# Issuing one small ones-matmul in front of a long V product instead of behind it, in a cached attention decode step

## The chip, the cores and the metric

The kernel runs on one core of one Trainium2 chip. The metric is the device time of one execution in microseconds (us). The profile's span of one execution is about 1.8 us shorter than that time. The record marks each run fast or slow by its time and granted clock.

## The reference, cut to what matters

```python
def _A_ref(x, k_cache, v_cache, wq, wo):      # B=2, Sq=1, D=512, 32 heads of Dh=128, Sk=8192, bf16
    q = (x @ wq) as heads
    scores = einsum("bhqd,bhkd->bhqk", q, k_cache) * (Dh ** -0.5)
    p = softmax(scores)
    o = einsum("bhqk,bhkd->bhqd", p, v_cache)
    return o as one row @ wo
h  = x + _A_ref(layernorm(x), ...)
h2 = h + gated_mlp(layernorm(h))              # F=1376
```

There is one query row for each of two batch rows, so every byte of the K and V caches (2 x 134 MB) is read once and used for very little arithmetic.

## The kernel before

The work is a loop over 32 "pairs": a pair is two heads of one batch row, 16 pairs to a row. Each pair has a K tile and a V tile of 4 MB each. All tiles come through one ring of 6 buffers, loaded by one issuing queue (SyncE).

```python
    def scores(n, between=None):               # VectorE, in place in the K tile
        ...
        nc.vector.tensor_tensor(out=kt, in0=kt, in1=qb, op=ALU.mult)
        if between is not None:
            between()
        width = Dh
        while width > 8:                       # four halving additions, then a reduction
            ...
        ... exp on ScalarE into pm[n % 3]; its sums go to zm[:, b, i, :]

    def weighted_v_moving(n):                  # TensorE: 32 matmuls on the V tile
        ...
        for g in range(T2 // TG):
            nc.tensor.matmul(out=o, lhsT=pm[...], rhs=vt[...], ...)
        ... copy by ScalarE, then 4 small matmuls into ob[b][:, i, :]

    def inverse_z(b, s, e):
        zb = ps_s.tile([P, e - s, 2], f32, tag="st", name="zb")
        nc.tensor.matmul(out=zb, lhsT=mean_f, rhs=zm[:, b, s:e, :], start=True, stop=True)
        nc.vector.reciprocal(out=zi[b][:, s:e, :], in_=zb)

    def first_row():                           # normalize batch row 0
        inverse_z(0, 0, NP)
        normalize(0, 0, NP, ob[0])

    load_k(0)
    for n in range(N - 2):                     # N = 32, NP = 16
        load_k(n + 1)
        load_v(n)
        scores(n, between=first_row if n == NP + 2 else None)
        weighted_v_moving(n)
```

The softmax denominators of batch row 0 are summed over partitions by `zb`, a matmul with a matrix of equal constants (the ones-matmul of the title). VectorE uses it in the middle of pair 18, between that pair's multiply and its additions. In TensorE's program order `zb` stands behind the V product of pair 17.

The softmax here doesn't subtract the row's maximum and nothing guards it: scores larger than these inputs give would overflow.

## Time and profile before

| | before |
|---|---|
| time, median | 667.52 us (667.27 to 667.75) |
| VectorE busy | 596.5 us, 90% of the span |
| TensorE busy | 340.3 us, 51% |
| queue of loads, packets' time | 99.1% of 16 engines' span |
| moved | 281.35 MB, mean 423 GB/s |

Two readings compete. These are rows of the page's forty equal slices (about 16.6 us each; a digit is the busy share in tenths) and the head of its chain of waits.

```profile
DVE  1699999999999999999999479999999999999941
...
DMA  9999999999999999999999999999999999999996
...
DVE 71%; DMA 22%; PE 4%; issue 2%; SPq 1%; ACT 0%; DVEq 0%; ACTq 0%
```

VectorE (DVE) has one visible hole, two slices wide, and the chain puts 71% on VectorE. Read alone, this says: VectorE is the limit, so fill the hole. The DMA row says something else: it never falls below 9 until the last slice. The list of VectorE's waits (total us, times, longest us) gives the hole a name:

```profile
DVE kv L173 <- DMA kv<-in_A_k_cache_dram: 17.7, 7, 13.7
DVE zi_224 L225 <- PE zb L224: 13.0, 1, 13.0
```

And this is TensorE's timeline around it (start us, duration us, then the instruction; in brackets the idle time before it and what ended it):

```profile
364.73 1.05 PE L213 MATMUL ob_221<-sel,osb 8*128 8x2 f32 x8 [0.74 <-ACT osb L211]
374.13 9.82 PE L207 MATMUL o<-kv,pm_87 128*8 128x512 bf16 x32 [8.35 <-DMA kv<-in_A_v_cache_dram]
384.69 1.05 PE L213 MATMUL ob_221<-sel,osb 8*128 8x2 f32 x8 [0.74 <-ACT osb L211]
385.67 0.41 PE L224 MATMUL zb<-zm,mean_f 128*128 128x32 f32 x2
```

TensorE idles 8.35 us for V of pair 17, multiplies for 9.82 us, and only then comes to `zb`, 0.41 us of work whose inputs were ready earlier. The Trainium skill, "PSUM — Partial Sum Buffer", section "Engine vs sequencer instructions", says that matmuls start and complete in program order; this trace agrees: `zb` starts at 385.67 us, behind the product. VectorE's multiplies and the reciprocal show the price:

```profile
344.95 8.69 DVE L173 TENSOR_TENSOR kv<-kv,qrep 128x16384 bf16<-128x16384 bf16 x1 [0.66 <-DMA kv<-in_A_k_cache_dram]
364.39 8.69 DVE L173 TENSOR_TENSOR kv<-kv,qrep 128x16384 bf16<-128x16384 bf16 x1 [0.66 <-DMA kv<-in_A_k_cache_dram]
386.11 0.36 DVE L225 RECIPROCAL zi_224<-zb 128x32 f32<-128x32 f32 x1 [13.02 <-PE zb L224]
396.58 8.68 DVE L173 TENSOR_TENSOR kv<-kv,qrep 128x16384 bf16<-128x16384 bf16 x1
415.27 8.68 DVE L173 TENSOR_TENSOR kv<-kv,qrep 128x16384 bf16<-128x16384 bf16 x1
```

In the six pairs up to the stall the starts are 19.44 us apart, with a short wait for K each time (earlier, VectorE catches up with the loads at 18.69 us a pair). After the stall they are 18.69 us apart, without a wait. The first figure is the pace of the loads, the second is VectorE's own. The table by stretches (start:end, length, busy us of PE, PEld, DVE, ACT and POOL with counts, granted clock, DMA share, GB/s) covers the time before, around and after the stall:

```profile
14.00:364.39 350.39, 181.93 (x734) 74.36 (x730) 332.76 (x108) 28.04 (x93) 0.00 (x0) 0.72 1.00 431
364.39:396.58 32.19, 12.25 (x50) 5.54 (x50) 18.92 (x9) 1.68 (x6) 0.00 (x0) 0.63 1.00 431
396.58:602.00 205.42, 111.02 (x440) 44.96 (x440) 202.78 (x67) 15.24 (x55) 0.00 (x0) 0.73 1.00 431
```

In the middle stretch VectorE is busy for 18.92 of 32.19 us, yet the loads run at the same 431 GB/s as everywhere else.

### The profile page before, as it was taken

To read this page: it belongs to the slowest core of one execution; us is meant where nothing else is said; L and a number is where in the kernel's file an instruction comes from. 1 tells how busy PE (TensorE), PEld (TensorE's weight loads), DVE (VectorE), ACT (ScalarE), POOL (GpSimd) and SP (SyncE) were. 2 spreads that over 40 slices of the span, in tenths; PEclk is the share of its full clock that TensorE was granted. 3 is DMA by queue.
4 is the path that set the end of the run, shared out by engine and by line. 5 is a ranking of instruction groups with operands and counts; after the bars stand their busy time and mean duration, and the time that the engine had idled before them with its cause. 6 is when DMAs were issued, how large, how long until landed. Compare 5 with 4: busy or idle time off the path is not lost.

```text
span 665.8 us, 4530 instructions
## 1 busy us (share of the span) xinstructions
PE 340.3 (51%) x1930; PEld 152.9 (23%) x1930; DVE 596.5 (90%) x221; ACT 53.2 (8%) x176; POOL 1.6 (0%) x11
## 2 busy tenths in 40 slices
PE   2344356654445665444656524656554445654284
PEld 1211122211122221112222111222211212212274
DVE  1699999999999999999999479999999999999941
ACT  2200000000000000000000000000000000000010
POOL 0000000000000000000000000000000000000000
PEclk9756787666678866677787568787765788766655
DMA  9999999999999999999999999999999999999996
GB/s 378 439 424 427 441 431 418 441 435 422 433 431 429 432 433 429 429 439 428 425 437 426 428 439 427 428 435 439 416 434 441 419 430 439 423 436 426 380 398 235
DMA packets 15020, 281.35 MB, mean 423 GB/s; under 512 B 1204, under 2 KB 5400, under 8 KB 6040
## 3 DMA queue, kind: packets, MB, share of 16 engines
q1 hardware_dynamic: 14996, 281.06, 99.1%
q8 instruction: 15, 0.25, 0.1%
q14 instruction: 5, 0.04, 0.0%
q10 hardware_dynamic: 4, 0.00, 0.0%
HBM read 281.05 MB, written 0.00 MB: 422 GB/s over the span
## 4 chain that ended last, share of the span: by engine, by line
DVE 71%; DMA 22%; PE 4%; issue 2%; SPq 1%; ACT 0%; DVEq 0%; ACTq 0%
DVE kv L179 34%; DVE kv L173 32%; DMA kv<-in_A_v_cache_dram 18%; DVE sc L187 4%; DMA kv<-in_A_k_cache_dram 3%; PE o L207 3%; SPq L159 1%; PE y_ps L326 0%; PE gate_ps L308 0%; PE up_ps L308 0%; PE o_b L219 0%; PE ob_221 L213 0%; DVE y_row L336 0%; PE ln2mu L99 0%; PE yt_ps L334 0%
## 5 line engine op out<-in xcount | busy, mean ns | idle before, releaser
L173 DVE TENSOR_TENSOR kv<-kv,qrep 128x16384 bf16<-128x16384 bf16 x32 | 277.9, 8684 | 17.7 <-DMA kv<-in_A_k_cache_dram 17.7
L179 DVE TENSOR_TENSOR kv<-kv 128x8192 bf16<-128x8192 bf16 (+3 forms) x128 | 276.2, 2158 | 4.3
L207 PE MATMUL o<-kv,pm_85 128*8 128x512 bf16 x320 | 92.3, 460 | 100.8 <-DMA kv<-in_A_v_cache_dram 60.9
L207 PE MATMUL o<-kv,pm_86 128*8 128x512 bf16 x320 | 92.6, 461 | 83.7 <-DMA kv<-in_A_v_cache_dram 67.6
L207 PE MATMUL o<-kv,pm_87 128*8 128x512 bf16 x320 | 89.3, 449 | 83.9 <-DMA kv<-in_A_v_cache_dram 67.9
L207 PEld LDWEIGHTS <-pm_85 128*8 128x8 bf16 x320 | 31.7, 100 | 157.6 <-issue 68.2
L207 PEld LDWEIGHTS <-pm_86 128*8 128x8 bf16 x320 | 31.9, 100 | 140.2 <-issue 74.9
L207 PEld LDWEIGHTS <-pm_87 128*8 128x8 bf16 x320 | 31.2, 98 | 137.8 <-issue 74.5
L211 ACT ACTIVATE osb<-o 8x512 f32<-8x512 f32 x30 | 17.6, 586 | 409.4 <-PE o L207 409.4
L187 DVE TENSOR_REDUCE sc<-kv 128x128 f32<-128x1024 bf16 x32 | 39.0, 1219 | 3.6 <-DVE kv L179 0.5
L213 PE MATMUL ob_220<-sel,osb 8*128 8x2 f32 x128 | 16.8, 248 | 11.8 <-ACT osb L211 11.8
L213 PEld LDWEIGHTS ob_220<-sel,osb 8*128 8x128 f32 x128 | 15.4, 186 | 19.9 <-ACT osb L211 18.6
L213 PE MATMUL ob_221<-sel,osb 8*128 8x2 f32 x112 | 14.7, 249 | 10.3 <-ACT osb L211 10.3
L213 PEld LDWEIGHTS ob_221<-sel,osb 8*128 8x128 f32 x112 | 13.5, 186 | 17.4 <-ACT osb L211 17.4
L192 ACT ACTIVATE pm_85<-sc 64x128 bf16<-64x128 f32 x22 | 7.6, 344 | 66.7 <-DVE sc L187 66.6
L192 ACT ACTIVATE pm_86<-sc 64x128 bf16<-64x128 f32 x22 | 7.6, 344 | 60.3 <-DVE sc L187 60.2
L139 PE MATMUL qps<-wq_sb,xnb 128*64 128x512 bf16 x64 | 9.4, 464 | 5.1 <-DMA wq_sb<-in_A_wq_dram 5.1
L225 DVE RECIPROCAL zi_224<-zb 128x32 f32<-128x32 f32 x1 | 0.4, 358 | 13.0 <-PE zb L224 13.0
L267 PEld LDWEIGHTS <-wo_sb 128*128 128x128 bf16 x256 | 8.9, 118 | 10.3 <-DMA wo_sb<-in_A_wo_dram 8.7
L192 ACT ACTIVATE pm_87<-sc 64x128 bf16<-64x128 f32 x20 | 6.9, 345 | 37.9 <-DVE sc L187 37.7
L267 PE MATMUL a_ps<-oc_222,wo_sb 128*128 128x1 bf16 x128 | 4.4, 172 | 8.5 <-DMA wo_sb<-in_A_wo_dram 8.5
L219 PEld LDWEIGHTS <-kv 128*128 128x128 bf16 x256 | 7.4, 105 | 4.7 <-issue 2.9
(73 smaller groups left out, 64.6 us busy)
## 6 DMA issues: line engine op xcount, KB each, us to landing
kv<-in_A_k_cache_dram SPq DMA_DIRECT2D x32, 4096.0 KB, 35.2
kv<-in_A_v_cache_dram SPq DMA_DIRECT2D x31, 4096.0 KB, 43.9
wq_sb<-in_A_wq_dram SPq DMA_DIRECT2D x1, 4096.0 KB, 12.5
wo_sb<-in_A_wo_dram SPq DMA_DIRECT2D x1, 4096.0 KB, 46.7
kv<-in_A_v_cache_dram SPq DMA_DIRECT2D x4, 1024.0 KB, 20.2
wgu<-in_B_W_gate_dram SPq DMA_DIRECT2D x1, 1376.0 KB, 27.3
wgu<-in_B_W_up_dram SPq DMA_DIRECT2D x1, 1376.0 KB, 27.2
wd_sb<-in_B_W_down_dram SPq DMA_DIRECT2D x1, 768.0 KB
```

The source lines that it names most:

```text
L139: nc.tensor.matmul(out=qps[half * HALF:(half + 1) * HALF], lhsT=xnb[:, b, c, :], rhs=wq_v[:, c, g * QP:(g + 1) * QP, half, :], start=(c == ...
L159: nc.sync.dma_start(out=t[:, j * step:(j + 1) * step, :], in_=src[:, j * step:(j + 1) * step, :])
L173: nc.vector.tensor_tensor(out=kt, in0=kt, in1=qb, op=ALU.mult)
L179: nc.vector.tensor_tensor(out=_view(kt, 0, [[Dh, T2], [1, half]]), in0=_view(kt, 0, [[Dh, T2], [1, half]]), in1=_view(kt, half, [[Dh, T2], ...
L187: nc.vector.tensor_reduce(out=sc, in_=_view(kt, 0, [[Dh, T2], [1, 8]]), axis=AXIS.X, op=ALU.add)
L192: nc.scalar.activation(out=pm[ps, :, half], in_=sc[ps, :], func=ACT.Exp, accum_out=zm[ps, b, i, half:half + 1], scale=SCALE)
L207: nc.tensor.matmul(out=o, lhsT=pm[:, ts, :].rearrange("p t two -> p (t two)"), rhs=vt[:, ts, :].rearrange("p t d -> p (t d)"), start=(g == ...
L211: nc.scalar.activation(out=osb, in_=o, func=ACT.Copy)
L213: nc.tensor.matmul(out=ob[b][:, i, :], lhsT=osb[:, j, :], rhs=sel[:, j, :], start=(j == 0), stop=(j == TG - 1))
L219: nc.tensor.matmul(out=o, lhsT=vt[:, t, :], rhs=pm[:, t, :], start=(t == 0), stop=(t == T2 - 1))
L225: nc.vector.reciprocal(out=zi[b][:, s:e, :], in_=zb)
L267: nc.tensor.matmul(out=a_ps[:, b, c:c + 1], lhsT=wo_v[:, h, :, c], rhs=oc[b][:, h // 2, h % 2:h % 2 + 1], start=(b == 0 and h == 0 and c = ...
```

## The change

The intent is to let the ones-matmul run in the time in which TensorE waits for V of pair 17 anyway, so that VectorE finds the sum ready in pair 18. Nothing is added or removed.

```diff
-    def inverse_z(b, s, e):
+    def sum_z(b, s, e):
         zb = ps_s.tile([P, e - s, 2], f32, tag="st", name="zb")
         nc.tensor.matmul(out=zb, lhsT=mean_f, rhs=zm[:, b, s:e, :], start=True, stop=True)
-        nc.vector.reciprocal(out=zi[b][:, s:e, :], in_=zb)
+        return zb
+
+    def inverse_z(b, s, e, zb=None):
+        nc.vector.reciprocal(out=zi[b][:, s:e, :], in_=zb or sum_z(b, s, e))
 ...
     def first_row():
-        inverse_z(0, 0, NP)
+        inverse_z(0, 0, NP, zb0)
 ...
         scores(n, between=first_row if n == NP + 2 else None)
+        if n == NP + 1:
+            zb0 = sum_z(0, 0, NP)
         weighted_v_moving(n)
```

## The prediction

> **What bounds the kernel now.** The load queue, over nearly the whole run, although VectorE looks busy (90% in the table of engines). The page's DMA part: 281.35 MB, queue packets filling 99.1% of sixteen engines' time. The table by stretches gives 431 GB/s at a DMA share of 1.00 in all three of: 14 to 364.39 us (before the stall that the change aims at), 364.39 to 396.58 us (around it), 396.58 to 602 us (after it). The stall does not show in the DMA. The Trainium skill, "DMA: Bandwidth & Descriptors", section "Where 436 GB/s comes from", puts the fabric's ceiling at 435.2 GB/s; 431 measured agrees, so there is no reserve.
>
> A pair is 8.39 MB, so 19.45 us at 431 GB/s (estimate). VectorE needs 18.69 us a pair (timeline; starts 396.58, 415.27, 433.95). From 248 to 364 us it starts each multiply after a 0.66 us wait for K, every 19.44 us: the load pace.
>
> **What the change touches.** VectorE has multiplied pair 18 by 373.1 us and then waits 13.0 us (list of waits) for the ones-matmul zb. That stands on TensorE behind pair 17's 32 V matmuls, which start when that V lands at 374.13 and last to 384, then the ScalarE copy (0.59) and 8 small matmuls (1.05); zb itself takes 0.41 us at 385.67. The change adds no instruction, byte or buffer. It puts zb right after the small matmuls that end at 365.8, into TensorE's 8.35 us idle before V of pair 17 lands. The first row's z is long complete. So the wait of 13.0 us goes to about 0; reciprocal (0.36) and normalize (0.19) stay. V products are not delayed.
>
> **How much is critical.** The chain of waits does not run through the stall here, but through two V loads of 48 us and their products. In before, the stall lets loads get ahead: after it VectorE runs 13 pairs at 18.69 without waiting for K. After the change it meets K just in time and waits about 0.7 us a pair, some 9 us over 13 pairs, given back. Its last multiply would start near 364.4 + 13 x 19.44 = 617.1 instead of 620.9 us, 3.8 us earlier. This does not shorten the end: the last V quarter lands at 651.0 us, 11 us after VectorE's last pair (639.6), then comes a fixed tail. Its landing is set by the bytes queued ahead. At 384 to 397 us several 4 MB loads are still queued, so the delayed issues never empty the queue; issuing earlier only makes loads wait longer in it.
>
> **Prediction.** 667.3 us, range 665.0 to 669.0 (before 667.52). Faster by over 2%: 0.03; within 2%: 0.95; slower by over 2%: 0.02.
>
> **What would show it.** Right: the zi wait of 13.0 us disappears; VectorE's wait for K grows from 17.7 us in 7 waits to 25 to 28 in about 20; multiply starts stay 19.4 us apart after pair 18; GB/s stays 431 in each stretch; median K issue-to-landing time grows from 35 towards 45 us; the last V quarter lands at 651 within 1 us. VectorE's last multiply starts 2 to 4 us earlier, without effect.
>
> Wrong: if the DMA rate rises above 431 after 396 us and the last V lands several us earlier, loads had reserve and the stall was critical; up to 13 us could go (654). If zb still waits (a dependence on the newest z accumulate or its PSUM buffer), nothing moves. If the deeper queue disturbs the order at the end (gate, up and down weights behind V), the tail could lengthen by 1 to 2 us.

## The result, and the profile after

The changed kernel takes 667.37 us (median, 667.23 to 667.40), against 667.52 us. The ratio is 0.9997 with a 95% interval of 0.998 to 1.0015. Ratios here are the mean time of one kernel's fast runs over that of the other's of the same rounds, so they are not quite the ratio of the medians.

The local effect is exactly what was intended. On TensorE, `zb` now runs at 364.90 us, and pair 17's product starts when its V lands, as before:

```profile
364.90 0.41 PE L224 MATMUL zb<-zm,mean_f 128*128 128x32 f32 x2
374.27 8.87 PE L207 MATMUL o<-kv,pm_87 128*8 128x512 bf16 x32 [8.96 <-DMA kv<-in_A_v_cache_dram]
```

VectorE's wait for `zb` in row 0 is gone from the list of waits, and the wait for K has grown from 17.7 us in 7 waits to this:

```profile
DVE kv L173 <- DMA kv<-in_A_k_cache_dram: 27.3, 21, 13.6
```

The reader sees the time going back in the starts of the multiplies:

```profile
364.53 8.69 DVE L173 TENSOR_TENSOR kv<-kv,qrep 128x16384 bf16<-128x16384 bf16 x1 [0.66 <-DMA kv<-in_A_k_cache_dram]
373.14 0.35 DVE L228 RECIPROCAL zi_224<-zb 128x32 f32<-128x32 f32 x1
383.98 8.69 DVE L173 TENSOR_TENSOR kv<-kv,qrep 128x16384 bf16<-128x16384 bf16 x1 [0.30 <-DMA kv<-in_A_k_cache_dram]
403.42 8.69 DVE L173 TENSOR_TENSOR kv<-kv,qrep 128x16384 bf16<-128x16384 bf16 x1 [0.66 <-DMA kv<-in_A_k_cache_dram]
422.86 8.69 DVE L173 TENSOR_TENSOR kv<-kv,qrep 128x16384 bf16<-128x16384 bf16 x1 [0.66 <-DMA kv<-in_A_k_cache_dram]
```

There is no hole any more, but the spacing is 19.44 us almost to the end (once it is 20.73). The last multiply starts at 618.79 instead of 620.85 us: of the 13 us only 2.1 arrive there, and they are of no use, because the kernel ends with the last quarter of V, which reaches TensorE at 651.14 us instead of 651.02. The first two lines are from before, the last two from after:

```profile
620.85 8.68 DVE L173 TENSOR_TENSOR kv<-kv,qrep 128x16384 bf16<-128x16384 bf16 x1
651.02 0.35 PE L219 MATMUL o_b<-pm_86,kv 128*128 128x2 bf16 x7 [1.67 <-DMA kv<-in_A_v_cache_dram]
...
618.79 8.69 DVE L173 TENSOR_TENSOR kv<-kv,qrep 128x16384 bf16<-128x16384 bf16 x1 [0.76 <-DMA kv<-in_A_k_cache_dram]
651.14 0.34 PE L219 MATMUL o_b<-pm_86,kv 128*128 128x2 bf16 x7 [1.86 <-DMA kv<-in_A_v_cache_dram]
```

Here is the same table by stretches, and the same rows of the page:

```profile
14.00:364.39 350.39, 179.70 (x738) 73.90 (x735) 332.74 (x108) 28.79 (x96) 0.00 (x0) 0.73 1.00 431
364.39:396.58 32.19, 13.70 (x55) 5.82 (x55) 31.47 (x10) 1.72 (x7) 0.00 (x0) 0.71 1.01 434
396.58:602.00 205.42, 110.88 (x434) 44.88 (x433) 194.17 (x66) 15.24 (x55) 0.00 (x0) 0.71 1.00 431
```

```profile
DVE  1699999999999999999999999999999998999931
...
DMA  9999999999999999999999999999999999999996
...
DMA 48%; DVE 47%; SPq 1%; PE 1%; issue 1%; DVEq 0%; ACT 0%
```

The chain of waits has changed from 71% VectorE and 22% DMA to 47% and 48%, while the time has not moved. Two resources whose paces differ by 4% (19.44 against 18.69 us a pair) each wait for the other somewhere, and following the chain back one step at a time jumps between them on waits of 0.66 us. Its shares are then no measure of what a saving is worth.

Loads are issued earlier and wait longer: the median time from issue to landing grew from 35.2 to 39.5 us for K and from 43.9 to 48.6 us for V.

### The profile page after: what moved, and what is told of

It is laid out like the page before. It is cut to its first block, busy times and chain, and to the rows that moved or that the text cites. A ratio compares the mean times of both kernels' runs of the same rounds, so it can differ in the third digit from the quotient of the medians.

```text
span 665.6 us, 4528 instructions
## 1 busy us (share of the span) xinstructions
PE 340.4 (51%) x1930; PEld 152.9 (23%) x1930; DVE 597.7 (90%) x221; ACT 53.2 (8%) x176; POOL 1.6 (0%) x11
## 2 busy tenths in 40 slices
DMA packets 15020, 281.35 MB, mean 423 GB/s; under 512 B 1204, under 2 KB 5400, under 8 KB 6040
## 4 chain that ended last, share of the span: by engine, by line
DMA 48%; DVE 47%; SPq 1%; PE 1%; issue 1%; DVEq 0%; ACT 0%
DMA kv<-in_A_k_cache_dram 45%; DVE kv L179 22%; DVE kv L173 22%; DMA kv<-in_A_v_cache_dram 4%; DVE sc L187 3%; SPq L159 1%; PE y_ps L331 0%; PE gate_ps L313 0%; PE up_ps L313 0%; PE o_b L219 0%; DVE y_row L341 0%; PE ln2mu L99 0%; PE yt_ps L339 0%; PE ln2var L108 0%; PE a_ps L272 0%
## 5 line engine op out<-in xcount | busy, mean ns | idle before, releaser
L173 DVE TENSOR_TENSOR kv<-kv,qrep 128x16384 bf16<-128x16384 bf16 x32 | 278.0, 8688 | 27.3 <-DMA kv<-in_A_k_cache_dram 27.3
L139 PEld LDWEIGHTS <-xnb 128*64 128x64 bf16 x64 | 5.1, 123 | 8.2 <-issue 5.0
## 6 DMA issues: line engine op xcount, KB each, us to landing
kv<-in_A_k_cache_dram SPq DMA_DIRECT2D x32, 4096.0 KB, 39.5
kv<-in_A_v_cache_dram SPq DMA_DIRECT2D x31, 4096.0 KB, 48.6
wgu<-in_B_W_up_dram SPq DMA_DIRECT2D x1, 1376.0 KB, 27.3
```

Of the source, the lines that this page charges most:

```text
L139: nc.tensor.matmul(out=qps[half * HALF:(half + 1) * HALF], lhsT=xnb[:, b, c, :], rhs=wq_v[:, c, g * QP:(g + 1) * QP, half, :], start=(c == ...
```

## The experiments

Theory A: the load queue works at its full rate all the time and sets the end; a pause of VectorE costs nothing as long as enough loads are queued and VectorE can catch up. Rival B: VectorE's time is critical, and the 13 us were lost elsewhere. Rival C: what limits the loads is not their bandwidth but how soon buffers come free.

### More pause: 21 and 42 extra reductions (e1, e2)

The pause is put back as work with thrown-away results, after the multiply of pair 18. It is longer than the old stall. The diff is cut: `junk` is a scratch tile.

```diff
         if between is not None:
             between()
+            if n == NP + 2:
+                for _ in range(21):        # 42 in e2
+                    nc.vector.tensor_reduce(out=junk, in_=_view(kt, 0, [[Dh, T2], [1, 8]]),
+                                            axis=AXIS.X, op=ALU.add)
```

> The changed kernel with 21 extra reductions of 1.22 us on VectorE (25.6 us, results thrown away) where the old stall was; the outputs stay right. Theory A (the load queue sets the end; a pause of VectorE is absorbed as long as loads are queued): VectorE loses 25.6 us at pair 18 but stops waiting for K for the rest, 8 to 9 us back; its last multiply starts near 633.5, its end (652) just passes the landing of the last V (651), so the time grows by 1 to 6 us, to 668 to 673; GB/s stays 431 until 600 us. Rival B (VectorE's time is critical, and the change's gain was lost elsewhere): 25 us more, near 693.

> The same with 42 extra reductions, 51 us. Theory A: about 30 us of loads lie queued ahead of the next one, so the queue now runs empty for some 15 to 25 us and VectorE ends long after the last V: 690 to 702, that is 23 to 35 us for 51 us of added work, and a visible fall of GB/s near 400 us. Rival B: 51 us more, near 719.

The 21 reductions took 26.3 us, and the kernel took 676.58 us: 9.1 us more than before. The 42 took 52.6 us, and the kernel 703.02 us: 35.5 us more, 1.0 us over the top of what was expected. Neither is what rival B says (the full 26 and 52 us). Between the two, 26.3 us of work cost 26.4 us, so past some knee every microsecond is paid. If a pause below the knee costs nothing, these two points put it at about 26.3 - 9.1 = 17.2 us of pause (an estimate, checked in e8), some 4 us more than the old stall of 13.0 us.

The table by stretches shows that in e1 the loads did not notice (lines of 374 to 414 us):

```profile
374.00:384.00 10.00, 9.75 (x32) 3.19 (x31) 9.73 (x9) 0.00 (x0) 0.00 (x0) 0.72 1.00 429
...
404.00:414.00 10.00, 3.12 (x8) 0.97 (x9) 9.79 (x6) 0.80 (x4) 0.00 (x0) 0.51 1.01 436
```

In e2 the queue did run dry, 40 to 50 us into a pause that began at 373.6 us:

```profile
404.00:414.00 10.00, 0.00 (x0) 0.00 (x0) 9.73 (x9) 0.00 (x0) 0.00 (x0) 0.50 1.00 429
414.00:424.00 10.00, 0.00 (x0) 0.00 (x0) 9.73 (x9) 0.00 (x0) 0.00 (x0) 0.50 0.66 285
424.00:434.00 10.00, 0.00 (x0) 0.00 (x0) 9.86 (x5) 0.00 (x0) 0.00 (x0) 0.50 0.00 0
434.00:444.00 10.00, 6.44 (x22) 2.27 (x23) 9.49 (x4) 0.80 (x4) 0.00 (x0) 0.64 0.68 263
```

So the queue holds out for well over 40 us without VectorE, more than the 30 us expected: TensorE finished pair 17 in the pause and freed one more buffer, and a K load went out at 384.0 us. What sets the knee is therefore not the queue running empty, but VectorE's own way to the end, and the tail on TensorE that follows it (e8, e9): with 26.3 us of pause VectorE never waits for K again and runs at 18.69 us a pair up to 653.3 us, after the last V has landed.

The larger miss is that of e1. There the last multiply starts at 634.16 us as expected (633.5), but 676.58 us is 3.6 us above the top of what was expected. The experiments e9 and e10 below ask why.

### The knee, checked (e8)

The same edit, with 13 reductions.

> 13 extra reductions at pair 18, 1.252 us each as measured in the 21-reduction run, so 16.3 us. From the two delay runs (26.3 us cost 9.1 us, 52.6 us cost 35.5 us, so every us past the knee is paid in full) the knee is at about 17.2 us. Theory A with that knee: 667.2 to 668.0, still free, with the last multiply of VectorE near 624.1. If instead the cost rises smoothly from zero (a share of every stall is paid): about 3 to 5 us, 670 to 672.

Measured: 668.57 us, ratio 1.0017 (1.0004 to 1.0029), for a pause of 16.3 us. The last multiply starts at 624.31 us, as expected. The total is 0.6 us over the top of the expectation and 1.4 us under the bottom of the smooth alternative, so the cost stays small up to the knee. The trace shows where the rest lies. In e8 TensorE no longer waits for the last V; it reaches the last 25 matmuls of the final V product at 651.35 us, and in the kernel before, where it does wait for V, at 651.37 us. So at 16.3 us VectorE's path has just drawn level with the loads. The excess of this trace is a gap that follows, for which the profile shows no releaser (first before, then e8):

```profile
652.67 0.81 PE L219 MATMUL o_b<-pm_86,kv 128*128 128x2 bf16 x25 [1.30 <-issue]
...
653.57 0.80 PE L223 MATMUL o_b<-pm,kv 128*128 128x2 bf16 x25 [2.22 <-issue]
```

The spans differ by 0.9 us (666.7 and 665.8), as the gaps do. e1 fits as well: its last multiply starts 9.85 us later than in e8, its gap is 0.60 us, and its span is 8.2 us longer, which is 9.85 less the 1.62 by which the gap is shorter. Read from the traces, the knee is thus at about 16 us, some 3 us above the old stall. Why the gap varies was not investigated. It stands at a fixed place: in the kernel before, the tail has gaps of 1.28, 1.51 and 1.30 us without a releaser, with 128 matmuls from each to the next. That TensorE waits there for its instructions (the page lists an instruction queue of 15 packets, 0.25 MB) is a guess that no run tested.

### Order on TensorE in the tail (e9, e10)

At the end of the kernel the same kind of ones-matmul stands in front of the V product of pair 30. It needs the last exponentials; the product does not.

```diff
-    inverse_z(L, NP - 1, NP)
     o_a = ps_o.tile([P, 1, 2], f32, tag="o", name="o_a")
     weighted_v_stationary(N - 2, o_a[:, 0, :], 0, T2)
+    inverse_z(L, NP - 1, NP)
     normalize(L, NP - 2, NP - 1, o_a)
```

> The 21-reduction kernel with the last pair's ones-matmul issued behind the V product of pair 30 instead of in front of it. The first 21-reduction run took 676.6 us, 3.6 us over the top of what was expected, because VectorE's end is followed by a serial tail in which that V product (3.41 us, 128 matmuls) waits in TensorE's order behind a ones-matmul that needs the last exponentials. If that explains the miss, 672.8 to 673.8 now. If the rest of the tail absorbs it, 676.6.

> The changed kernel with the same reorder at its end and no extra work. There the last V quarter lands at 651.1 us, after that product is done (644), so under theory A the time stays: 667.2 to 667.6. If the order on TensorE in the tail counts even here, up to 3.4 us faster, 664.

With the pause of e1, the reorder brought 676.58 down to 673.36 us, inside what was expected. TensorE's timeline of e1, and then of e9:

```profile
654.18 0.59 PE L228 MATMUL zb<-zm,mean_f 128*128 128x2 f32 x2 [6.94 <-ACT pm L196]
654.63 3.55 PE L223 MATMUL o_a<-pm,kv 128*128 128x2 bf16 x128
```

```profile
647.01 3.16 PE L223 MATMUL o_a<-pm,kv 128*128 128x2 bf16 x113
...
654.09 0.59 PE L228 MATMUL zb<-zm,mean_f 128*128 128x2 f32 x2 [1.31 <-ACT pm L196]
```

In e1 the product of pair 30 sits behind a wait of 6.94 us; in e9 it runs inside that wait. This accounts for 3.2 of the 3.6 us by which e1 missed. It also moves the knee: with this order the same pause costs 673.36 - 667.41 = 5.95 us instead of 9.1 (667.41 is e10, below). Without the pause (e10) the same reorder gave 667.41 us, ratio 0.9998 (0.9986 to 1.0011): nothing, because the last V quarter lands after that product either way. This is the studied change in small: a reorder on TensorE is worth its time only where the path that it shortens, and not the load queue, ends last.

### Less work for VectorE (e3)

The first of the four halving additions is left out, so VectorE sums half of the products. The arithmetic is wrong; the comparison with the reference passed all the same, so it says nothing about this part.

```diff
-        width = Dh
+        width = Dh // 2
```

> The changed kernel without the first of the four halving additions (4.44 us a pair, 142 us in all; the scores are then of half of the products only, so the output is wrong on purpose). VectorE needs 14.25 us a pair. Theory A: the time stays, 665 to 668, and VectorE's wait for K grows by over 100 us. Rival B: far faster, below 600.

Measured: 667.57 us, ratio 1.0000 (0.9983 to 1.0016). VectorE's busy time fell from 597.7 to 457.1 us, 141 us less, and not one of them reached the total. They went here:

```profile
DVE kv L173 <- DMA kv<-in_A_k_cache_dram: 159.8, 30, 13.4
```

This is the plainest verdict against rival B.

### Fewer bytes, in both orders (e4, e5)

The V loads of pairs 20, 22, 24 and 26 are left out; those products read the spent K tile. The output is wrong, and the comparison passed here too. The edit also holds those K tiles until their products are done, in both kernels alike. e4 has the changed order, e5 the order before.

```diff
+    SKIP = (20, 22, 24, 26)
 ...
-        load_v(n)
+        if n in SKIP:
+            vts[n] = kts[n]
+        else:
+            load_v(n)
```

> The changed kernel with the V loads of pairs 20, 22, 24 and 26 left out (16.8 MB, 38.9 us at 431 GB/s; those products read the spent K tile instead, so the output is wrong on purpose). VectorE's work is unchanged. Theory A: with the queue relieved the end is set by VectorE, running at 18.69 us a pair from about pair 20: last multiply near 610, total near 649 (646 to 653). Theory B (VectorE critical throughout): no change, 667. Its twin in the old order (next call): theory A expects near 660, so that the same change is worth about 11 us there.

> The kernel before, with the same four V loads left out (wrong output on purpose). Theory A: the 13.0 us stall at pair 18 is now on VectorE's path, its last multiply stays at 620.9 and the total is 656 to 662, 9 to 13 us over the twin in the changed order. Rival B (moving the ones-matmul never frees VectorE, the time is paid elsewhere in its own or TensorE's work): both twins alike within 2 us.

Measured: 651.49 us in the changed order and 661.42 us in the old one, 9.9 us apart. (They ran on different chips; the kernel before, run beside each, took 667.53 and 667.40 us. The trace of e5 is of its slowest run, 662.62 us.) So bytes do count, and with the load queue relieved the very same change is worth 1.5% (9.9 of 661.4 us). VectorE's list of waits in e5 still has the stall (12.9 us of it in row 0):

```profile
DVE kv L173 <- DMA kv<-in_A_k_cache_dram: 17.7, 8, 13.3
DVE zi L225 <- PE zb L224: 14.4, 2, 12.9
```

What differs from the kernel before is not the loads' rate during the stall, but their rate after it. These are stretches of e5, with the same bounds as above:

```profile
364.39:396.58 32.19, 12.10 (x50) 5.49 (x50) 18.93 (x9) 1.66 (x6) 0.00 (x0) 0.68 1.01 433
396.58:602.00 205.42, 110.92 (x440) 44.39 (x440) 202.78 (x67) 15.26 (x55) 0.00 (x0) 0.73 0.95 398
```

In e5 the last multiply starts at 620.82 us, in e4 at 609.65 us: 11.2 us of the saved wait now arrive at the end of VectorE's work. The total of e4 is 2.5 us over the central estimate of 649, inside the range given.

### Fewer buffers, in both orders (e6, e7)

```diff
-    ring = ctx.enter_context(tc.tile_pool(name="ring", bufs=6))
+    ring = ctx.enter_context(tc.tile_pool(name="ring", bufs=5))
```

> The changed kernel with 5 load buffers in place of 6. Theory A (bandwidth of the queue limits): three loads are still queued, the queue never empties, so 666 to 671 (the weights at the end may come some us later). Rival C (what limits is how soon buffers come free, not the bandwidth): a sixth of the depth gone makes it over 5% slower, above 700. Expected median time of K from issue to landing under A: about 10 us less, near 30.

> The kernel before with 5 buffers. Theory A: a 13 us pause still finds about 20 us of loads queued ahead, so within 2 us of its twin in the changed order. If the reserve is smaller than that, it is slower than the twin by the part that isn't covered, up to 13 us.

Measured: 667.40 us in the changed order and 667.45 us in the old one. Rival C falls: a sixth of the ring can go without a trace in the time, and the 13 us stall (13.1 us in this run of the old order) still hides. One expectation missed its place: the median K landing time stayed (39.5 to 38.8 us), and it was V's that shrank, from 48.6 to 29.7 us. How far the ring can shrink before the stall shows was not tried.

## Why the prediction was right, point by point

- **The load queue is the limit.** Right. 141 us less VectorE work changed nothing, one ring buffer of six could go, and 16.8 MB fewer bytes gave 15.9 us (667.37 to 651.49) before VectorE became the limit. The rate stayed as predicted (431, 434 and 431 GB/s in the three stretches).
- **The wait of 13.0 us goes to about 0, V products are not delayed.** Right: `zb` at 364.90 us, pair 17's product at 374.27 instead of 374.13 us.
- **Given back as waits for K.** Right: 27.3 us in 21 waits, predicted 25 to 28 in about 20. Starts 19.44 us apart after pair 18, as predicted, but for the one named next.
- **Last multiply 2 to 4 us earlier, without effect.** Right at the lower edge: 2.1 us. One K wait of 1.95 us late in the loop (before the multiply at 560.36 us) accounts for 1.3 of the 1.7 us missing from 3.8.
- **The end is fixed by the last V.** Right: 651.14 against 651.02 us.
- **K's landing time towards 45 us.** Right in direction, too large: 39.5 us. This is not because the median takes in pairs in which nothing changed: for the loads issued from 370 to 600 us alone it is 39.5 us too, against 33.6 before. The change only keeps K's landing time at what it is from 260 to 364 us in both kernels (39.5), and the prediction does not say where 45 came from.
- **Several loads queued, so the delayed issues never empty the queue.** Right. The experiments add how much margin there was, which the prediction did not work out: the loads themselves would have lasted over 40 us, but VectorE's own end allowed a pause of about 16 to 17 us, so a stall of 13 us was safe by only 3 to 4.

No run here that does all of the work beats both kernels by more than noise. From the stretches, 281.35 MB at 431 GB/s alone take 653 us (an estimate), of 665.6 us of span, so what does not lower the bytes or raise that rate can win 1.9% at the very most.

## What to carry to other kernels

Before paying for a hole in a busy engine's row, look at the row of the resource that feeds it, during that hole and from there to the end: if the loads keep their full rate all the way (here 431 GB/s), the engine will meet them again later and give the time back. Their rate during the hole alone does not decide it: in e5 it was 433 GB/s there, but 398 afterwards, and filling the hole won 9.9 us. The chain of waits and a 90% busy share cannot tell apart two resources whose paces lie within some per cent; the spacing of repeated instructions before and after a stall can (19.44 us fed by loads, 18.69 us on its own). Keep such a reorder if it is free, because it starts to pay as soon as the bytes shrink: with four V loads fewer it was worth 9.9 us.

## What the Trainium skill lacked or had wrong

- "DMA: Bandwidth & Descriptors", section "Where 436 GB/s comes from", says that for HBM to SBUF the HBM side (about 358 GB/s) binds. This program, on one core, moved 431 GB/s for hundreds of microseconds, 99% of the 435.2 GB/s that the same section gives for the fabric. The sentence by itself lacks a qualification that stands elsewhere: above that section the page calls its measurements single-core numbers, and "HBM Reference", section "Specifications (TRN2)", says that a core streaming alone measures about 425.
- "Perfetto Trace Analysis", section "Optimization Strategy", says that consistent bubbles can mean too few buffers. Here the repeating 0.66 us bubble on VectorE was that of a saturated load queue: 5 buffers instead of 6 gave 667.40 us, the same time, with 27.3 us of waits for K in 20 places. That passage names no other cause.
- "Perfetto Trace Analysis" does not say how much of an engine's pause a queue of loads absorbs. Here, with 4 MB loads, 16.3 us cost 1.0 us, 26.3 us cost 9.1 us and 52.6 us cost 35.5 us.
